# Decay rows of an mLSTM block loaded as two half loads per head group, under a new written order

## The chip, the cores and the metric

One Trainium2 chip (trn2), one of its cores. The metric is the time of one execution on the device, in microseconds (us). Of the kernel before, three timed runs gave 303.72, 299.47 and 302.79 us: the median is 302.79 us. One more execution was profiled; its own time is given further below.

## The reference, cut to what matters

Three layers in a row: an mLSTM attention with a matrix state for each of 2 batches and 8 heads (768 steps, head size 40), a feed-forward layer on the normalised result, and a gated convolutional feed-forward layer. All in float32.

```python
for t in range(S):                                    # attention, S = 768
    m_new = np.maximum(f_gate[:, :, t] + m, i_gate[:, :, t])
    f_stab = np.exp(f_gate[:, :, t] + m - m_new)
    i_stab = np.exp(i_gate[:, :, t] - m_new)
    C = f_stab * C + i_stab * outer(vt, kt);  n = f_stab * n + i_stab * kt
    y[:, :, t] = sigmoid(o_gate) * (C @ qt) / maximum(abs(n @ qt), 1)
x = y as (2, 768, 320)
x = x + relu(layernorm(x) * g @ w_ch1) @ w_ch2        # 320 -> 1280 -> 320
h = relu(x @ w_in)                                    # 320 -> 1024
out = (h * sigmoid(conv3(h, conv_w))) @ w_out         # 1024 -> 320
```

## The kernel before, in words

The sequence is cut into six chunks of 128 steps (c = 0 to 5). Within a chunk the recurrence is a masked attention, and what came before it enters through a carried state, so a chunk of a batch b is one "group" (c, b). Three stages run as a pipeline over chunks: the attention of chunk c, the first feed-forward layer f1 of chunk c (five units u, L605), and the second layer f2 of chunk c - 3 (L666).

A group (c, b) in `attention` (L415) does, in the order of its code:

- L420 loads the block `vk` (values, keys, output gate; 484 KB) and L431 the block `xy` (keys and queries, 512 KB). Both have three buffers that go around.
- For c >= 2, L451 loads the weights `wt` of the group from the small DRAM tensor `gd` (gate sums, written once at L337) by broadcasting eight rows to 128 partitions (512 KB); POOL masks it (L453) and ACT takes eight exponentials (L457).
- For c >= 2, L472 and L473 load `eg`, the decay rows, also from `gd`: partitions 0 to 63 get four rows of 128 numbers (heads 0 to 3 of the batch), partitions 64 to 127 the next four. The source is an access pattern of two blocks of 64 equal rows, and it is one load (256 KB, 128 pieces of 2,048 B). ACT takes its exponential in place (L474). `eg` has two buffers, one for each batch. For c = 1 the rows come from TensorE instead (L467, L470).
- POOL multiplies the queries by `eg` (L476, tile `qt`), and later the carried state by the last column of `eg` (L565, tile `ctmp`). After these two the buffer of `eg` is free for the group (c + 1, b).
- TensorE makes the scores (L491), VectorE multiplies them by `wt` (L498), TensorE makes numerator and norm from state and values (L517, L520), and the keys' product for the new state (L558); VectorE adds that to `ctmp` (L566), which is the state of (c + 1, b).
- VectorE and ACT normalise, and TensorE transposes the result (L579) for f1. An f1 unit is sixteen matmuls (L592 to L596), a relu on ACT (L616), a remainder on VectorE (L618) and twelve matmuls (L601 to L603). f2 is built of the same two helpers.

The order of all work is written out by hand. `Sched` (L84) only collects the operations in the order of the code and numbers them, 0 to 1294. `ORDER` (L32) is a list of these numbers, and the instructions are emitted in that order; a "-" in it is a dummy matmul on TensorE (L805), of which there are 52. If the list is no permutation, or if it breaks a dependency, the order of the code is used (L132). Each engine works off its own instructions strictly in this order. All loads and stores go out through one queue, SP's (L256 for loads): an issue that waits there, for a buffer to come free, holds back every later issue. Weights come in 640 KB blocks (L357) through staging buffers, are put together by ACT, VectorE and POOL (L343 to L346) and split in two parts (L369 to L391).

Of the kernel before, what the change touches and what calls it, by code (L numbers as in the profile page):

```python
# [13 lines left out]
AF = mybir.ActivationFunctionType  # L14
# [3 lines left out]
L = 128  # L18
# [11 lines left out]


ORDER = """  # L32
13 6 12 11 4 10 5 38 82 29 2 37 28 8 15 91 98 16 27 3 9 17 19 20 21 18 22 107 25 23 26 - - - - - - - - - - - - - -
49 24 163 30 84 164 14 83 32 31 85 114 39 33 86 34 46 40 87 41 47 48 42 88 - - - 52 43 36 50 44 51 92 35 53 54 93 55
7 56 - - - - 67 94 57 45 62 99 63 95 74 100 58 59 60 64 68 65 89 66 61 96 - - - - - - - 76 101 165 108 90 69 123 109
70 102 287 71 166 168 167 72 103 169 97 73 77 - - - - - - - - - - - - - - - - 79 110 130 171 170 80 299 0 78 111 173
298 115 81 - - - - - - 175 286 - - 292 177 116 174 184 172 388 176 104 112 288 105 75 113 256 289 106 146 124 117
# [43 lines left out]
"""  # L81


# [58 lines left out]
def tile_kernel(ctx, tc, gf, gf80, kq0, vko, gln, w1, w2, win, wout, cw, out):  # L142
# [5 lines left out]
    op = sch.op  # L148
# [58 lines left out]
    ctmp = ctm[0:104, 0:164].rearrange("p (j e) -> p j e", j=4)  # L207
    negm = ctm[:, 0:256].bitcast(BF16).rearrange("p (k t) -> p k t", k=4)
# [38 lines left out]
    def da(n, psum=False):  # L247
        return 120 + (0 if psum else 45) + 0.72 * n

    def dg(n):  # L250
        return 80 + 2.3 * n
# [163 lines left out]
    def attention(c, b, to_xt):  # L415
# [43 lines left out]
        if c:  # L459
            if c == 1:  # L460
                gk, gb = pbank("sm")

                def feg():
                    for j in range(4):
                        for h2 in range(2):
                            r = r0 + 4 * h2 + j
                            pe.matmul(out=gb[64 * h2:64 * h2 + 64, j * L:(j + 1) * L], rhs=g80[0:16], start=True, stop=True,  # L467
                                      lhsT=ident[0:16, r:r + 1].to_broadcast([16, 64]))
                op(P, 1036, ["g80", "ident"], [gk], feg, act=0.5)
                op(A, da(512, True), [gk], [ek], lambda: ac.activation(out=e, in_=gb.rearrange("p (j t) -> p j t", j=4), func=AF.Exp))  # L470
            else:
                gsrc = gd[r1:r1 + 8, :].rearrange("(i j) t -> i (j t)", i=2).unsqueeze(1).to_broadcast([2, 64, 4 * L])  # L472
                load(e, gsrc, [ek], 128 * 2048 + 1, reads=["gd"])  # L473
                op(A, da(512), [], [ek], lambda: ac.activation(out=e, in_=e, func=AF.Exp))  # L474
            op(G, dg(512), [ek, (xkk, 0), (xkk, 1)], [qk],
               lambda: gq.tensor_tensor(out=q[0:104], in0=xt[0:104, 1, :].rearrange("p (j t) -> p j t", j=4), in1=e[0:104], op=ALU.mult))  # L476
        if c < NC - 1:
            op(A, 130, [(wk, h) for h in range(8)], [dk], lambda: ac.activation(out=d.unsqueeze(2), in_=w[:, :, L - 1:L], func=AF.Copy))
# [69 lines left out]
        if c < NC - 1:  # L548
# [12 lines left out]
            if c == 0:  # L561
                op(V, dv(164), [sk], [ck], lambda: ve.tensor_copy(out=cb[0:104], in_=sv))
            else:
                op(G, dg(164), [ek, ck], ["ctmp", "negm"],
                   lambda: gq.tensor_tensor(out=ctmp, in0=cb[0:104], in1=e[0:104, :, L - 1:L].to_broadcast([104, 4, D + 1]), op=ALU.mult))  # L565
                op(V, dv(164), [sk, "ctmp"], [ck], lambda: ve.tensor_tensor(out=cb[0:104], in0=sv, in1=ctmp, op=ALU.add))  # L566
        yield
# [300 lines left out]
```

## Time and profile of the kernel before

| what | value |
|---|---|
| timed runs, us | 303.72, 299.47, 302.79; median 302.79 |
| the profiled execution, us | 299.37 |
| its span, first to last instruction, us | 297.6 |
| TensorE busy (matmul) | 277.1 us, 93% |
| VectorE, ACT, POOL busy | 193.1 us, 178.7 us, 101.7 us |
| bytes moved by DMA | 33.17 MB, 111 GB/s over the span |
| mean granted TensorE clock | 0.986 |

How to read it: 297.6 us is the time between the first and the last instruction, and 1.8 us of the execution lie outside it. TensorE's share counts the dummies too, and the ends of matmuls are modelled, so "busy" can hide small waits. The clock is a share of full speed, 1.00 being 2.4 GHz. In the rows, PE is TensorE, PEld its weight loads, DVE VectorE, ACT ScalarE, POOL GpSimd, SP the queue that issues DMA.

### The profile page before, as it was taken

Reading aid. Unit: us, or ns where it says so; the run is one execution under the profiler, and the core shown is the slowest. Engines: PE = TensorE matmul, PEld = TensorE weight load, DVE = VectorE, ACT = ScalarE, POOL = GpSimd, SP = SyncE. Lnnn points to the kernel's source line nnn. Section 1 sums busy time; section 2 is a strip of 40 time slices with the busy share of each in tenths; the row PEclk is TensorE's granted clock in tenths of the full one; section 3 lists DMA queues with packets and bytes.
Section 4 is the critical chain, followed back from the end, with each engine's and each line's share of the span. In section 5 each row is a group of like instructions: output and inputs, shape, how many; then the busy total and the mean of one; then the engine's idle time right before and its main releaser. Section 6 shows DMA issues by size and latency. Waiting matters only on the chain.

```text
span 297.6 us, 7323 instructions
## 1 busy us (share of the span) xinstructions
PE 277.1 (93%) x2972; PEld 254.6 (86%) x2975; DVE 193.1 (65%) x415; ACT 178.7 (60%) x409; POOL 101.7 (34%) x152
## 2 busy tenths in 40 slices
PE   8999999898985797979999799999999999999995
PEld 3756899888884796968999699999999999999994
DVE  5597579539960579656693566857354468777573
ACT  3875796776871905954555743455344347787473
POOL 2331865496543925517120060001000200434540
PEclk9999999999999599999999999999999999999998
DMA  7958746983456257300425000000001000010012
GB/s 274 343 206 319 324 162 209 312 273 107 161 173 191 94 213 224 132 31 9 166 74 154 21 0 25 24 3 0 2 0 46 0 0 2 2 40 6 2 45 88
DMA packets 10514, 33.17 MB, mean 111 GB/s; under 512 B 1216, under 2 KB 3040, under 8 KB 10480
## 3 DMA queue, kind: packets, MB, share of 16 engines
q1 hardware_dynamic: 10480, 32.71, 32.2%
q8 instruction: 23, 0.38, 0.6%
q14 instruction: 11, 0.09, 0.1%
HBM read 30.70 MB, written 2.01 MB: 110 GB/s over the span
## 4 chain that ended last, share of the span: by engine, by line
PE 59%; DMA 17%; DVE 11%; ACT 5%; issue 3%; POOL 2%; SPq 0%; DVEq 0%; POOLq 0%; ACTq 0%
DMA eg<-gd 17%; PE bk L601 7%; PE bk L603 7%; PE bk L602 7%; PE bk L592 6%; PE bk L593 6%; PE bk L594 6%; PE bk L805 3%; PE bk L491 3%; PE bk L595 3%; PE bk L596 3%; PE bk L520 2%; DVE wt L498 2%; PE bk L517 2%; DVE scr L716 1%
## 5 line engine op out<-in xcount | busy, mean ns | idle before, releaser
L716 DVE SCALAR_TENSOR_TENSOR scr<-scr,cwr 128x256 f32<-128x256 f32 x70 | 34.4, 527 | 15.3 <-ACT scr L710 15.1
L601 PE MATMUL bk<-w2h,uh 128*128 128x320 f32 x120 | 39.1, 326 | 0.0
L603 PE MATMUL bk<-w2h,ul 128*128 128x320 f32 x120 | 37.8, 315 | 0.2 <-DVE ul L618 0.2
L602 PE MATMUL bk<-w2l,uh 128*128 128x320 f32 x120 | 37.7, 314 | 0.0
L592 PE MATMUL bk<-xth,w1h 128*128 128x256 f32 x120 | 35.3, 295 | 1.9 <-DVE ul L618 1.9
L618 DVE SCALAR_TENSOR_TENSOR ul<-bk,uh 128x512 fp32r<-128x512 f32 x30 | 20.5, 686 | 22.7 <-ACT uh L616 22.4
L594 PE MATMUL bk<-xtl,w1h 128*128 128x256 f32 x120 | 33.8, 282 | 0.0
L593 PE MATMUL bk<-xth,w1l 128*128 128x256 f32 x120 | 33.7, 281 | 0.0
L592 PE MATMUL bk<-rh,wih 128*128 128x256 f32 (+1 forms) x96 | 28.2, 294 | 2.5 <-DVE ul L618 2.1
L593 PE MATMUL bk<-rh,wil 128*128 128x256 f32 (+1 forms) x96 | 27.2, 283 | 0.0
L594 PE MATMUL bk<-rl,wih 128*128 128x256 f32 (+1 forms) x96 | 27.1, 283 | 0.0
L616 ACT ACTIVATE uh<-bk 128x512 fp32r<-128x512 f32 x30 | 17.7, 590 | 15.6 <-PE bk L596 11.5
L691 POOL COPY scr<-scr 128x8 f32<-128x8 f32 (+1 forms) x21 | 4.3, 216 | 65.2 <-DVE scr L721 54.6
L592 PEld LDWEIGHTS bk<-xth,w1h 128*128 128x128 f32 x120 | 22.5, 188 | 3.1 <-DVE ul L618 2.3
L346 POOL TENSOR_TENSOR scr<-scr 128x640 int32<-128x640 int32 x14 | 18.2, 1302 | 20.4 <-DVE scr L345 15.2
L498 DVE TENSOR_TENSOR wt<-bk,wt 128x512 f32<-128x512 f32 x24 | 15.5, 684 | 13.9 <-PE bk L491 6.1
L457 ACT ACTIVATE wt<-wt,bcol 128x128 f32<-128x128 f32 x64 | 22.9, 390 | 2.4 <-POOL wt L453 2.4
L601 PEld LDWEIGHTS bk<-w2h,uh 128*128 128x128 f32 x120 | 23.1, 192 | 0.8 <-issue 0.2
L603 PEld LDWEIGHTS bk<-w2h,ul 128*128 128x128 f32 x120 | 23.1, 192 | 0.4 <-DVE ul L618 0.4
L601 PE MATMUL bk<-woh,uh 128*128 128x320 f32 x74 | 23.3, 315 | 0.0
L602 PEld LDWEIGHTS bk<-w2l,uh 128*128 128x128 f32 x120 | 23.1, 193 | 0.0
L603 PE MATMUL bk<-woh,ul 128*128 128x320 f32 x74 | 23.0, 310 | 0.0
(185 smaller groups left out, 813.9 us busy)
## 6 DMA issues: line engine op xcount, KB each, us to landing
xy<-in_kq_dram SPq DMA_DIRECT2D x12, 512.0 KB, 6.5
vk<-in_vko_dram SPq DMA_DIRECT2D x12, 484.0 KB, 8.6
wt<-gd SPq DMA_DIRECT2D x8, 512.0 KB, 3.8
scr<-in_w_dram SPq DMA_DIRECT2D x6, 640.0 KB, 6.4
stg<-in_w_dram SPq DMA_DIRECT2D x4, 640.0 KB
scr<-in_win_dram SPq DMA_DIRECT2D x4, 640.0 KB, 11.4
scr<-in_wout_dram SPq DMA_DIRECT2D x4, 640.0 KB, 4.0
eg<-gd SPq DMA_DIRECT2D x8, 256.0 KB
```

The source lines that it names most:

```text
L346: op(G, 80 + 1.78 * n, [(rk, 0)], [(rk, 1)], lambda: gq.tensor_tensor(out=hi, in0=hi, in1=lo, op=ALU.add))
L457: lambda h=h: ac.activation(out=w[:, h, :], in_=w[:, h, :], func=AF.Exp, bias=bcol[:, c * 16 + r0 + h:c * 16 + r0 + h + 1]))
L498: lambda wv=wv, pb=pb: ve.tensor_tensor(out=wv, in0=pb.rearrange("p (h t) -> p h t", h=4), in1=wv, op=ALU.mult))
L592: pe.matmul(out=pv, lhsT=wh[:, k, fs], rhs=hi(k), start=(k == 0), stop=False)
L593: pe.matmul(out=pv, lhsT=wl[:, k, fs], rhs=hi(k), start=False, stop=False)
L594: pe.matmul(out=pv, lhsT=wh[:, k, fs], rhs=lo(k), start=False, stop=False)
L601: pe.matmul(out=a, lhsT=hi(b), rhs=wh[:, k, :], start=first, stop=False)
L602: pe.matmul(out=a, lhsT=hi(b), rhs=wl[:, k, :], start=False, stop=False)
L603: pe.matmul(out=a, lhsT=lo(b), rhs=wh[:, k, :], start=False, stop=last)
L616: op(A, da(512, True), [pk], [hk], lambda: ac.activation(out=uh[i], in_=pb, func=AF.Relu))
L618: lambda: ve.scalar_tensor_tensor(out=ul[i], in0=pb, scalar=0.0, in1=uh[i].bitcast(F32), op0=ALU.max, op1=ALU.subtract))
L716: lambda k=k, j=j: ve.scalar_tensor_tensor(out=cvt()[:, j], in0=h[:, j, :, k:k + 128], scalar=cw_t[:, k, f0 + j:f0 + j + 1], in1=cvt()[:, ...
```

## The change: what it does

The load of `eg` (L473) becomes two loads of 64 partitions each, one for each half of the heads. Each takes four consecutive rows of `gd` as one row of 512 numbers and broadcasts it to 64 partitions. The tile's dependency key is split in two halves; the exponential at L474, the product at L476 and the product at L565 use both halves. Bytes, values and the two buffers stay as they are. There are eight such groups, so eight loads more; the operations are now numbered 0 to 1302, and `ORDER` is a new list of them with 54 dummies.

```diff
-            op(A, da(512, True), [gk], [ek], lambda: ...)
+            op(A, da(512, True), [gk], [(ek, 0), (ek, 1)], lambda: ...)
...
             else:
-                gsrc = gd[r1:r1 + 8, :].rearrange("(i j) t -> i (j t)", i=2).unsqueeze(1).to_broadcast([2, 64, 4 * L])
-                load(e, gsrc, [ek], 128 * 2048 + 1, reads=["gd"])
-                op(A, da(512), [], [ek], lambda: ac.activation(out=e, in_=e, func=AF.Exp))
-            op(G, dg(512), [ek, (xkk, 0), (xkk, 1)], [qk],
+                for h2 in range(2):
+                    gsrc = gd[r1 + 4 * h2:r1 + 4 * h2 + 4, :].rearrange("j t -> (j t)").partition_broadcast(64)
+                    load(e[64 * h2:64 * h2 + 64].rearrange("p j t -> p (j t)"), gsrc, [(ek, h2)], 64 * 2048 + 1, reads=["gd"])
+                op(A, da(512), [], [(ek, 0), (ek, 1)], lambda: ac.activation(out=e, in_=e, func=AF.Exp))
+            op(G, dg(512), [(ek, 0), (ek, 1), (xkk, 0), (xkk, 1)], [qk],
...
-                op(G, dg(164), [ek, ck], ["ctmp", "negm"],
+                op(G, dg(164), [(ek, 0), (ek, 1), ck], ["ctmp", "negm"],
...
-49 24 163 30 84 164 14 83 32 31 85 114 39 33 86 34 46 40 87 41 47 48 42 88 - - - 52 43 36 50 44 51 92 35 53 54 93 55
+49 24 163 30 84 164 14 83 32 31 85 114 39 33 86 46 40 34 87 41 299 47 48 42 88 - - - 52 43 36 50 44 51 92 35 53 54
...
+155 317 318 149 135 268 408 319 320 150 269 141 326 309 266 136 270 137 151 138 321 271 308 194 401 391 274 409 322
```

What the new order does with the parts that matter here, read from the two lists with the groups written as (c, b):

- Start. The new list keeps the first twelve issues of SP. The `xy` block of (1, 1) moves three places up, ahead of the third block of `w2`; the loads of `vk` for (1, 0) and (2, 0) and of the convolution's weights (L769) also come ahead of the fourth blocks of `w1` and `w2`, and that of `vk` for (1, 1) comes later. On TensorE the first f1 unit has two dummies more ahead of it, and the rest of its sequence up to the end of chunk 1 is the same but for neighbours that change places.
- SP around chunks 2 and 3. Before: `wt` (2,0), `eg` (2,0), `wt` (2,1), `vk` (2,1), `xy` (2,0), `xy` (2,1), `eg` (2,1), and later `eg` (3,1), `eg` (3,0). After: `wt` (2,0), `xy` (2,1), second half of `eg` (2,0) (number 401), `wt` (2,1), first half of `eg` (2,0) (400), both halves of (2,1) (419, 420), the first half of (3,0) (522), then `vk` of (2,1) (407). In the same way both halves of `eg` (4,0) stand ahead of `vk` (3,0).
- POOL. `ctmp` of (2,0) (number 448) moves from behind the two key products L480 of chunk 2 to a place ahead of the query product L476 of (2,1). In chunks 3 and 4 the batch 0 pairs L476 and L565 move up in a like way, ahead of the masks L453 that follow.
- ACT. The exponential L474 of a group stands behind its loads by a stretch of other work in both lists; for (3, 0), (3, 1) and (4, 0) the new one has it ahead of more of the L457 exponentials of its group than before.
- TensorE. The groups' scores, numerators and transposes come at nearly the same places among the units of f1 and f2, mostly one to four operations earlier or later; the number and the size of matmuls is the same.
- End. The units of f2 for chunks 3 to 5 change places among themselves.

## Rows read from the trace of the kernel before

**Rows 1.** Page: the granted clock in 40 slices of the span.
```profile
PEclk9999999999999599999999999999999999999998
```

**Rows 2.** Stretches: length, busy PE, PEld, DVE, ACT, POOL, clock, DMA share, GB/s.
```profile
0.00:45.00 45.00, 43.27 (x432) 30.57 (x436) 31.47 (x82) 31.47 (x62) 19.23 (x27) 1.00 0.74 271
45.00:184.00 139.00, 124.10 (x1613) 116.16 (x1615) 89.67 (x188) 83.51 (x212) 62.12 (x86) 0.98 0.42 137
184.00:290.00 106.00, 105.64 (x928) 104.56 (x915) 69.34 (x140) 61.14 (x129) 20.34 (x39) 1.00 0.04 12
97.80:104.70 6.90, 6.37 (x60) 5.81 (x60) 2.77 (x5) 6.13 (x15) 5.67 (x10) 0.51 0.28 92
```

**Rows 3.** Timeline of TensorE: start, length, instruction, idle before it and its releaser.
```profile
68.07 0.68 PE L517 MATMUL bk<-c,qt 40*64 40x41 f32 x32 [1.08 <-DVE wt L498]
...
98.33 2.08 PE L491 MATMUL bk<-xy 40*128 40x128 f32 x16 [5.28 <-DVE wt L498]
...
118.59 0.87 PE L579 MATMUL bk<-ident,xc 128*128 128x128 f32 x6 [1.35 <-DVE c L566]
...
133.50 0.39 PE L592 MATMUL bk<-rh,wih 128*128 128x260 f32 x1 [1.68 <-DVE ul L618]
...
168.59 0.39 PE L592 MATMUL bk<-xth,w1h 128*128 128x256 f32 x1 [1.43 <-DVE ul L618]
```

**Rows 4.** Timeline of ACT at three of the loads, the same columns.
```profile
65.37 0.63 ACT L474 ACTIVATE eg<-eg 128x512 f32<-128x512 f32 x1 [1.55 <-DMA eg<-gd]
...
95.25 0.63 ACT L474 ACTIVATE eg<-eg 128x512 f32<-128x512 f32 x1 [6.21 <-DMA eg<-gd]
95.78 0.58 ACT L616 ACTIVATE uh<-bk 128x512 fp32r<-128x512 f32 x1
...
130.67 0.63 ACT L474 ACTIVATE eg<-eg 128x512 f32<-128x512 f32 x1 [1.74 <-DMA eg<-gd]
...
132.15 0.57 ACT L616 ACTIVATE uh<-bk 128x512 fp32r<-128x512 f32 x1
```

**Rows 5.** Chain that ended last: start, length; first and last of four such pieces.
```profile
51.58 13.77 DMA eg<-gd
...
156.51 8.02 DMA eg<-gd
```

**Rows 6.** Busy time by stretch, as rows 2: only eg loads, only wt loads.
```profile
140.30:142.10 1.80, 1.38 (x11) 1.38 (x12) 1.80 (x6) 0.01 (x1) 0.00 (x0) 1.00 0.13 49
147.20:149.60 2.40, 2.40 (x32) 1.97 (x33) 1.35 (x4) 0.78 (x2) 1.10 (x1) 1.00 0.54 213
```

**Rows 7.** DMA issues: count, KB, us to landing; 115.5 to 135 us, then all.
```profile
xy<-in_kq_dram SPq DMA_DIRECT2D x1, 512.0 KB, 15.6
...
vk<-in_vko_dram SPq DMA_DIRECT2D x12, 484.0 KB, 8.6
wt<-gd SPq DMA_DIRECT2D x8, 512.0 KB, 3.8
...
out_dram<-scr SPq DMA_DIRECT2D x12, 160.0 KB, 1.8
```

**Rows 8.** Instructions on eg: count, ns least/median/most, first and last start.
```profile
L256 SPq DMA_DIRECT2D eg<-gd x8: 497/514/644, 43.5 to 156.5; - x8
```

**Rows 9.** Chain that ended last: a run of sixteen dummies.
```profile
20.55 3.60 PE bk L805 x16
```

**Rows 10.** Timeline of POOL and TensorE near the numerators of chunk 2.
```profile
70.19 0.46 POOL L565 TENSOR_TENSOR ctmp<-c,eg 104x164 f32<-104x164 f32 x1
...
71.70 0.68 PE L517 MATMUL bk<-c,qt 40*64 40x41 f32 x32
```

**Rows 11.** Timeline of VectorE and POOL ahead of the wait at 118.59 us.
```profile
112.98 0.54 DVE L545 SCALAR_TENSOR_TENSOR xc<-x,mv,gln 128x320 f32<-128x320 f32 x1
...
115.27 3.02 DVE L545 SCALAR_TENSOR_TENSOR xc<-x,mv,gln 128x320 f32<-128x320 f32 x1
...
115.63 1.09 POOL L453 TENSOR_SCALAR_AFFINE_SELECT wt<-wt 128x1024 f32<-128x1024 f32 x1
```

More of the change, by code (lines that the diff above doesn't have):

```diff
@@ L32 @@
 ORDER = """
-13 6 12 11 4 10 5 38 82 29 2 37 28 8 15 91 98 16 27 3 9 17 19 20 21 18 22 107 25 23 26 - - - - - - - - - - - - - -
-49 24 163 30 84 164 14 83 32 31 85 114 39 33 86 34 46 40 87 41 47 48 42 88 - - - 52 43 36 50 44 51 92 35 53 54 93 55
-7 56 - - - - 67 94 57 45 62 99 63 95 74 100 58 59 60 64 68 65 89 66 61 96 - - - - - - - 76 101 165 108 90 69 123 109
-70 102 287 71 166 168 167 72 103 169 97 73 77 - - - - - - - - - - - - - - - - 79 110 130 171 170 80 299 0 78 111 173
-298 115 81 - - - - - - 175 286 - - 292 177 116 174 184 172 388 176 104 112 288 105 75 113 256 289 106 146 124 117
[43 rows of a table removed]
+13 6 12 4 10 11 5 38 82 29 2 37 28 8 15 91 98 16 27 3 9 17 19 20 21 18 22 107 25 23 26 - - - - - - - - - - - - - -
+49 24 163 30 84 164 14 83 32 31 85 114 39 33 86 46 40 34 87 41 299 47 48 42 88 - - - 52 43 36 50 44 51 92 35 53 54
+93 - - - - 57 55 7 56 94 45 62 67 99 63 95 74 58 59 60 64 68 65 - - - - 165 89 66 90 96 61 76 123 101 178 100 69 286
+77 70 388 102 108 166 287 71 167 168 109 75 72 110 73 115 169 - - - - - - - - - - - - - - - - - - 79 170 177 78 111
+173 171 80 116 172 174 112 81 250 - - - - - - - - - - - 288 97 103 292 113 130 124 104 175 184 256 289 105 126 125
[43 rows of a table added]
 """
@@ L469, in attention @@
                 op(P, 1036, ["g80", "ident"], [gk], feg, act=0.5)
-                op(A, da(512, True), [gk], [ek], lambda: ac.activation(out=e, in_=gb.rearrange("p (j t) -> p j t", j=4), func=AF.Exp))
+                op(A, da(512, True), [gk], [(ek, 0), (ek, 1)], lambda: ac.activation(out=e, in_=gb.rearrange("p (j t) -> p j t", j=4), func=AF.Exp))
             else:
-                gsrc = gd[r1:r1 + 8, :].rearrange("(i j) t -> i (j t)", i=2).unsqueeze(1).to_broadcast([2, 64, 4 * L])
-                load(e, gsrc, [ek], 128 * 2048 + 1, reads=["gd"])
-                op(A, da(512), [], [ek], lambda: ac.activation(out=e, in_=e, func=AF.Exp))
-            op(G, dg(512), [ek, (xkk, 0), (xkk, 1)], [qk],
+                for h2 in range(2):
[3 more added lines that the diff above has]
+            op(G, dg(512), [(ek, 0), (ek, 1), (xkk, 0), (xkk, 1)], [qk],
                lambda: gq.tensor_tensor(out=q[0:104], in0=xt[0:104, 1, :].rearrange("p (j t) -> p j t", j=4), in1=e[0:104], op=ALU.mult))
```

85 rows, old and new, of the table ORDER are left out of this document.

## The prediction

> **What bounds the kernel now.** I read the page first, then the windows by stretch, then TensorE's timeline for its waits, then ACT's at the same times, and last the chain of waits and the DMA.
>
> From 184 to 290 us TensorE is busy for 105.64 of 106 us [rows 2]: nothing but its own work bounds that stretch, and the change removes no matmul. From 0 to 45 us the loads set the pace (DMA share 0.74) and dummies fill TensorE. What can be won lies between 45 and 184 us: TensorE is busy for 124.10 of 139 us, so it waits for 14.9 us [rows 2]. The granted clock shows one dip there [rows 1]: from 97.8 to 104.7 us it is 0.51, which is the 1.2 GHz level of the two, 1.2 and 2.4 GHz [rows 2], right after TensorE's longest wait, 5.28 us up to 98.33 [rows 3].
>
> Four of the twelve waits that make up the 14.9 us go back to the `eg` load. The wait of 5.28 us is for L498, which waits for ACT's exponentials; ACT had stood still for 6.21 us until `eg` landed, and its queue then began with L474 [rows 3, 4]. Likewise 1.08 us at 68.07 behind L474 at 65.37, and 1.68 us at 133.50 behind L474 at 130.67 through the relu L616 at 132.15 [rows 3, 4]. The wait of 1.43 us at 168.59 is of the same kind: L474 began only when `eg`, issued at 156.51, had landed 8.02 us later [rows 3, 5]. Together 1.08 + 5.28 + 1.68 + 1.43 = 9.47 us. The other eight sum to 14.9 - 9.47 = 5.4 us; the largest, 1.35 us at 118.59 [rows 3], has nothing to do with `eg` (rival 2).
>
> Why is the load slow? The chain that ended last holds four of these loads, 13.77 us the first and 8.02 us the last [rows 5]. While only an `eg` load was in the DMA engines their share was 0.13, which is 2 of 16, at 49 GB/s; while only a `wt` load ran it was 213 GB/s and 0.54 on the mean of a stretch with its start and tail [rows 6]. 256 KB at 49 GB/s are 5.3 us, and two groups' loads in a row 10.7 us. Others suffer as well: an `xy` load issued right behind two `eg` loads took 15.6 us to land, against 3.8 us for a `wt` load of the same size [rows 7].
>
> **The change part by part.** *Half loads.* No row shows a load of 64 partitions. The nearest from below is an output store of 160 KB, 1.8 us, from above a `wt` load of 512 KB, 3.8 us, whose source is a broadcast of the same tensor in the same manner [rows 7]; at the far end the halves still run on two engines and the pair takes the 8.02 us of today [rows 5]. I take 2.5 us, since 128 KB is nearer to the store, and 0.5 us more for the second issue: the group lands 3 us after its first issue in place of 8 to 14.
>
> The Trainium skill, page "DMA: Bandwidth & Descriptors", section "Why a DMA increments its semaphore by 16 and not by 1", says that a load is dealt to the largest number of engines, up to 16, that divides the slowest dimension of both its sides. That is 2 for the old pattern, which the 0.13 of [rows 6] agrees with, and 16 for the new one, which no run here shows yet. Against the split speaks the page "SBUF — State Buffer", sections on the port swizzle and on issuing two DMAs to hit both halves: 64 partitions reach half of the ports, and two such loads one after the other do not add up. By its 196 GB/s for 64 partitions the pair would take an estimated 1.3 us in the engines, where its 436 GB/s for all ports would give 0.6; that is under 1 us for a group, and the sum would stay within 1 us of what follows unless several of these stood on the path.
>
> *What goes.* The four waits, 9.47 us, and the dip of the clock behind the longest one: 6.9 us at 0.51 did what takes 6.9 x 0.51 = 3.5 us, so 3.4 us. Together 12.9 us. Bounds: 0, if the load was not the last to come, and 14.9 + 3.4 = 18.3 us, if no wait at all is left.
>
> *What is late next.* In the place of each removed wait the next latest thing shows. The other eight waits have a mean of 5.4 / 8 = 0.68 us; four of these are 2.7 us. Bounds 0 and 9.47.
>
> *Added issues.* Eight more issues on SP, each of about 0.51 us [rows 8], 4 us in all. SP only issues and nothing computes on it, so they are hidden unless a load is due within half a microsecond; then 0.5 us each, 4 us at most, less than nothing if a half lands before its partner did. I take 0. The exponential's second semaphore and the doubled keys add nothing to ACT and POOL: the same instructions run.
>
> *Dummies.* Two more ahead of the first f1 unit. Sixteen in a row take 3.60 us, so 0.225 us each [rows 9]: 0.45 us if that stretch waits for them, 0 if it waits for loads anyway. I take 0.45.
>
> *The new order at the start and the end.* Up to 45 us the loads set the pace, at 271 GB/s [rows 2]. Some blocks change places; about 1 MB put ahead of a needed block (`vk` and `xy`, 996 KB) delays it by 1.0 MB / 271 GB/s = 3.8 us, and the needed one put ahead gains as much. From both sides: -3.8 to +3.8 us; I take 0, since the same blocks come before the end of chunk 1 in both orders. At the end the f2 units change places on a TensorE that is busy for 99.7% [rows 2]: 0, give or take 1 us.
>
> Sum, on the profiled execution: 299.37 - 12.9 + 2.7 + 0.45 = 289.6 us. The three timed runs lie 0.1 to 4.35 us above the profiled execution's 299.37 us, their median 3.4 us. Some of that spread may be the clock's dip itself, so I add half of it, 1.7 us: 291.3 us, 3.8% under 302.79. About 2% either way, 6 us, is what a measurement of this kernel tells from no change.
>
> **The rivals.** *1. The split does not spread.* The pair stays on two engines, 8.02 us or more a group [rows 5]. For it: no row shows such a load. Against: `wt` is broadcast in the same manner and is fast [rows 7]. Then only the new order and the dummies count: 299.37 + 0.45 + 1.7 = 301.5 us.
>
> *2. The load hid other waits.* With `eg` early, ACT, VectorE and POOL are as late. For it: ACT was busy for 6.13 of 6.9 us after the long wait [rows 2], so much of its work was only waiting its turn; and one VectorE instruction, L545, took 3.02 us against 0.54 when POOL's L453 and its neighbours ran beside it, after which TensorE waited 1.35 us [rows 3, 11]; the new order puts POOL's products in other places and may make more of these. Against: in its 6.21 us ACT had nothing else to do [rows 4], so that work does move up. If half of the 9.47 us stays and the clock still dips behind the longest one: 299.37 - 4.7 + 0.45 + 1.7 = 296.8 us, just at 2%.
>
> *3. SP is blocked, and it ends slower.* In the new order the first half of `eg` (3,0) is issued ahead of `vk` (2,1), and both halves of (4,0) ahead of `vk` (3,0). These halves wait until POOL has done L565 of the group before, which frees the buffer; `vk` is queued behind them, and the numerator L517 waits for `vk`. For it: before, L565 of (2,0) ran at 70.19 us, only 1.5 us ahead of L517 of (2,1) at 71.70 [rows 10], and a `vk` load takes 8.6 us [rows 7]. At that lateness `vk` lands at 70.65 + 0.5 + 8.6 = 79.7 us, TensorE waits 8 us, and the clock falls behind it as it did before: 8 + 3.4 = 11.4 us a place, two places 22.8 us: 291.3 + 22.8 = 314.1 us; at one place alone 302.7 us. It decides when L565 starts later than some 9 us before its numerator. Against: the new list has POOL do L565 of (2,0) ahead of the second query product, thus well ahead of the numerators, and with the two busy engines gone a `vk` load should take nearer to 4 us (the `wt` row) than 8.6.
>
> **How the numbers follow.** Forecast 0.62, rival 1 0.06, rival 2 0.19, rival 3 0.13 (0.08 at two places, 0.05 at one). Faster by over 2% (under 296.7 us): 0.62 and half of rival 2, 0.71. Within 2%: rival 1, the other half of rival 2, rival 3 at one place, 0.06 + 0.09 + 0.05 = 0.20, and 0.01 for an unlucky start: 0.21. Slower: rival 3 at two places, 0.08. The range: at the low end all waits and the dip are gone, 299.37 - 18.3 + 0.45 = 281.5, and half a microsecond for what lies outside, 282; at the high end it takes in rivals 1 and 2, 302. What is left out is rival 3 and a lucky start below 282, under 2 in 10.
>
> **What would show each step.** Right: the `eg` loads land within about 3 us, `xy` and `vk` in 4 to 6; the chain of waits holds no piece of 8 us for `eg`; the window from 45 us until the attention of chunk 5 is over has TensorE waits of 6 to 9 us in all; the clock has no dip to 0.5 there; ACT nowhere stands still for 6 us until `eg` lands. Wrong: TensorE waits ended by `vk`, or by VectorE's L498 behind a late `wt`; a low clock behind a new wait; landings of `eg` still at 8 us with a DMA share of 0.13; or a first f1 unit that starts several microseconds later than before.

## The result, and the profile after

The changed kernel took 285.42 us (median of four runs, 284.53 to 287.46), against 302.15 us for the kernel before in the same series (299.47 to 303.72). The ratio is 0.946, with a 95% interval from 0.938 to 0.955: faster by some 5%. The profiled execution took 287.46 us, its span is 285.7 us. The forecast was 291.3 us.

In the rows of the changed kernel, line numbers behind L473 are one higher than before (the exponential is L475, the query product L477, scores L492, numerators L518 and L521, transposes L580).

The page of the changed kernel: engines' busy time, the granted clock in 40 slices, the chain that ended last, and the issues of `eg`. These answer to the table ahead of the prediction and to [rows 1, 5, 7].

```profile
span 285.7 us, 7333 instructions
...
PE 274.7 (96%) x2975; PEld 254.2 (89%) x2977; DVE 190.4 (67%) x415; ACT 178.7 (63%) x409; POOL 102.7 (36%) x152
...
PEclk9998999979999999999999999999999999999999
...
PE 82%; DVE 13%; ACT 2%; issue 2%; POOL 0%; DVEq 0%
...
vk<-in_vko_dram SPq DMA_DIRECT2D x12, 484.0 KB, 6.1
...
eg<-gd SPq DMA_DIRECT2D x16, 128.0 KB, 4.0
```

The chain that ended last had four pieces of 8 to 15 us in which it only waited for `eg`; now no DMA is in it at all, and TensorE's part is 82% (59% before). A half load lands 4.0 us after its issue (median), a `vk` load after 6.1 us where it took 8.6.

TensorE's timeline of the changed kernel, every wait over 0.3 us between 45 and 184 us; it answers to [rows 3].

```profile
57.88 1.37 PE L580 MATMUL bk<-ident,xc 128*128 128x128 f32 x6 [1.86 <-DVE c L567]
...
77.85 0.82 PE L559 MATMUL bk<-vk 128*40 128x41 f32 x32 [0.87 <-DVE x L534]
...
87.39 0.55 PE L580 MATMUL bk<-ident,x 128*128 128x128 f32 x3 [0.66 <-DVE xtl L585]
...
111.79 0.55 PE L580 MATMUL bk<-ident,xc 128*128 128x128 f32 x3 [0.38 <-DVE c L567]
```

Busy time by stretch of the changed kernel, columns as in [rows 2].

```profile
0.00:45.00 45.00, 42.48 (x424) 29.41 (x427) 30.87 (x79) 30.44 (x62) 19.51 (x28) 0.96 0.77 274
45.00:184.00 139.00, 135.03 (x1823) 128.35 (x1822) 99.66 (x220) 91.32 (x228) 61.62 (x86) 0.99 0.42 137
...
58.10:61.50 3.40, 3.40 (x17) 3.40 (x16) 1.46 (x4) 1.78 (x7) 0.00 (x0) 0.50 0.02 5
```

Between 45 and 184 us TensorE now waits for 139 - 135.03 = 4.0 us, where it was 14.9 [rows 2]. None of the four waits that go back to `eg` is left. That is the 10.9 us of which the span's 297.6 - 285.7 = 11.9 us mostly consist. The dip of the clock behind the long wait is gone too, but this execution has two others, one of 3.4 us at 0.50 among the dummies and one, in the last row, behind the wait of 1.86 us. Two of the other three runs had a mean clock of 1.00 and took 285.79 and 284.53 us.

### The profile page after: what moved, and what is told of

Same layout as the page of the kernel before. It is cut to its first block, busy times and chain, and to the rows that moved or that the text cites. A ratio compares the mean times of both kernels' runs of the same rounds, so it can differ in the third digit from the quotient of the medians.

```text
span 285.7 us, 7333 instructions
## 1 busy us (share of the span) xinstructions
PE 274.7 (96%) x2975; PEld 254.2 (89%) x2977; DVE 190.4 (67%) x415; ACT 178.7 (63%) x409; POOL 102.7 (36%) x152
## 4 chain that ended last, share of the span: by engine, by line
PE 82%; DVE 13%; ACT 2%; issue 2%; POOL 0%; DVEq 0%
PE bk L602 10%; PE bk L604 10%; PE bk L603 9%; PE bk L593 8%; PE bk L595 8%; PE bk L594 8%; PE bk L806 5%; PE bk L492 4%; PE bk L596 4%; PE bk L597 4%; PE bk L521 3%; PE bk L580 3%; PE bk L518 2%; DVE xc L546 1%; DVE wih L380 1%
## 5 line engine op out<-in xcount | busy, mean ns | idle before, releaser
L717 DVE SCALAR_TENSOR_TENSOR scr<-scr,cwr 128x256 f32<-128x256 f32 x70 | 33.7, 516 | 17.0 <-ACT scr L711 16.8
L604 PE MATMUL bk<-w2h,ul 128*128 128x320 f32 x120 | 37.2, 310 | 0.0
L692 POOL COPY scr<-scr 128x8 f32<-128x8 f32 (+1 forms) x21 | 7.5, 362 | 67.4 <-DVE scr L722 56.8
L499 DVE TENSOR_TENSOR wt<-bk,wt 128x512 f32<-128x512 f32 x24 | 15.6, 684 | 11.7 <-PE bk L492 11.5
L594 PEld LDWEIGHTS bk<-xth,w1l 128*128 128x128 f32 x120 | 22.9, 191 | 0.0
L457 ACT ACTIVATE wt<-wt,bcol 128x128 f32<-128x128 f32 x64 | 22.4, 396 | 0.9 <-POOL wt L453 0.8
L595 PEld LDWEIGHTS bk<-xtl,w1h 128*128 128x128 f32 x120 | 22.9, 191 | 0.0
```

What stands on the lines that cost most here:

```text
L457: lambda h=h: ac.activation(out=w[:, h, :], in_=w[:, h, :], func=AF.Exp, bias=bcol[:, c * 16 + r0 + h:c * 16 + r0 + h + 1]))
L499: lambda wv=wv, pb=pb: ve.tensor_tensor(out=wv, in0=pb.rearrange("p (h t) -> p h t", h=4), in1=wv, op=ALU.mult))
L594: pe.matmul(out=pv, lhsT=wl[:, k, fs], rhs=hi(k), start=False, stop=False)
L595: pe.matmul(out=pv, lhsT=wh[:, k, fs], rhs=lo(k), start=False, stop=False)
L604: pe.matmul(out=a, lhsT=lo(b), rhs=wh[:, k, :], start=False, stop=last)
L717: lambda k=k, j=j: ve.scalar_tensor_tensor(out=cvt()[:, j], in0=h[:, j, :, k:k + 128], scalar=cw_t[:, k, f0 + j:f0 + j + 1], in1=cvt()[:, ...
```

## The experiments

Theory A: the cause is that the old load runs on two DMA engines. Theory B: the cause is the new order. Theory C: it helps to have two loads, whatever their engines.

**e1: the new order with the old load.** Both places of a pair stay in the order; the one load is issued at the earlier of them, the other place is empty.

```diff
+                first = {(2, 0): 1, (2, 1): 0, (3, 0): 0, (3, 1): 1, (4, 0): 1, (4, 1): 0, (5, 0): 0, (5, 1): 1}[c, b]
                 for h2 in range(2):
-                    gsrc = gd[r1 + 4 * h2:r1 + 4 * h2 + 4, :].rearrange("j t -> (j t)").partition_broadcast(64)
-                    load(e[64 * h2:64 * h2 + 64].rearrange("p j t -> p (j t)"), gsrc, [(ek, h2)], 64 * 2048 + 1, reads=["gd"])
+                    gsrc = gd[r1:r1 + 8, :].rearrange("(i j) t -> i (j t)", i=2).unsqueeze(1).to_broadcast([2, 64, 4 * L])
+                    op(SP, 460, ["gd"], [(ek, h2)], (lambda gsrc=gsrc: sp.dma_start(out=e, in_=gsrc)) if h2 == first else (lambda: None), ...)
```

> The new order, with each pair of half loads put back to the one old load of 128 partitions (issued where the first half stands; the other place is left empty). Theory A, the load's two DMA engines are the cause: most of the gain is lost, 297 to 304 us, with TensorE waits of over 8 us between 45 us and the end of chunk 5's attention and ACT waiting for the decay rows. Theory B, the new order is the cause: 285 to 290 us. Both in part: about 292 us.

Measured: 290.27 us, ratio 0.969 (0.964 to 0.973). Well over half of the gain is there with the old load. Theory A as stated falls: the slow load alone is not what costs the time. One piece of `eg` is left in the chain that ended last, where there were four: ACT stood still until it landed, and TensorE waited behind that. ACT, then TensorE, in e1 (lines two higher than in the changed kernel):

```profile
63.90 0.63 ACT L477 ACTIVATE eg<-eg 128x512 f32<-128x512 f32 x1 [2.99 <-DMA eg<-gd]
```

```profile
68.80 0.68 PE L520 MATMUL bk<-c,qt 40*64 40x41 f32 x32 [2.26 <-DVE wt L501]
```

**e2: the old order with the half loads,** both issued one behind the other in the old load's place.

```diff
-                load(e, gsrc, [ek], 128 * 2048 + 1, reads=["gd"])
+                def halves():
+                    for h2 in range(2):
+                        gsrc = gd[r1 + 4 * h2:r1 + 4 * h2 + 4, :].rearrange("j t -> (j t)").partition_broadcast(64)
+                        sp.dma_start(out=e[64 * h2:64 * h2 + 64].rearrange("p j t -> p (j t)"), in_=gsrc)
+                op(SP, 460, ["gd"], [ek], halves, dma=128 * 2048 + 1)
```

> The old order, with both half loads issued one right after the other in the place of the old load. Theory A: 285 to 291 us, the four TensorE waits at 68, 98, 133 and 169 us (9.5 us in all) gone or under 1 us each, and no dip of the clock behind the second. Theory B: 298 to 304 us.

Measured: 288.41 us, ratio 0.961 (0.956 to 0.966). Theory B as stated falls as well: either part alone gives the larger part of the gain. TensorE's timeline of e2 (lines three higher than in the changed kernel), from 85 to 135 us:

```profile
90.04 1.16 PE L495 MATMUL bk<-xy 40*128 40x128 f32 x16 [1.14 <-DVE rl L588]
...
107.19 0.38 PE L596 MATMUL bk<-xth,w1h 128*128 128x256 f32 x1 [0.52 <-DVE ul L622]
...
111.60 0.88 PE L583 MATMUL bk<-ident,xc 128*128 128x128 f32 x6 [1.35 <-DVE c L570]
...
120.99 0.41 PE L607 MATMUL bk<-w2h,ul 128*128 128x320 f32 x1 [0.16 <-DVE ul L622]
...
131.94 0.39 PE L596 MATMUL bk<-rh,wih 128*128 128x260 f32 x1 [0.44 <-DVE ul L622]
```

The wait of 1.35 us stands at the same transposes as in [rows 3], unchanged, and the kernel before had the other four of these too, each within 0.02 us. Between the first two rows it also had the wait of 5.28 us; that is gone, and of the four `eg` waits none is left. This is the clean test of the prediction's list of causes.

**e3: the changed kernel, with each half load on two engines.** The source has the same 64 equal rows, written as two blocks of 32.

```diff
-....rearrange("j t -> (j t)").partition_broadcast(64)
+....rearrange("j t -> (j t)").unsqueeze(0).unsqueeze(0).to_broadcast([2, 32, 4 * L])
```

> The changed kernel, but each half load reads a source pattern of two blocks of 32 equal rows in place of 64 equal rows: the same two loads, bytes and pieces of 2,048 B. Theory A, with the slowest dimension of the pattern setting the number of engines: two engines again, DMA share 0.13 while only such a load runs, and 295 to 304 us. Theory C, that it is the split into two loads which helps, whatever their engines: 284 to 288 us. If the two blocks are joined on the way the share is near 1 and the time that of the changed kernel.

Measured: 297.82 us, ratio 0.995 (0.992 to 0.998). Theory C falls: two loads without more engines bring nearly nothing. The stretch of e3 in which only such loads ran, then a wait of TensorE, then the load in the chain that it followed:

```profile
151.30:156.40 5.10, 3.12 (x25) 2.87 (x23) 1.93 (x5) 1.38 (x4) 1.14 (x1) 1.00 0.13 51
```

```profile
158.13 0.58 PE L593 MATMUL bk<-rh,wih 128*128 128x260 f32 x1 [3.71 <-ACT scr L693]
```

```profile
146.01 11.06 DMA eg<-gd
```

A share of 0.13 is 2 of 16 engines, as in [rows 6], at 51 GB/s. The last half was issued at 146.01 us, behind two others on the same two engines, took 11.06 us, and TensorE waited.

**e6: e1 with the load at the later place.** The only difference to e1 is which of the two places is empty.

```diff
-... if h2 == first else (lambda: None)
+... if h2 != first else (lambda: None)
```

> The new order with the one old load, now issued where the later of the two halves stands, up to some 20 us later for the groups of chunk 5. If the new order helps because it issues the decay rows earlier: 295 to 299 us, like the two halves on two engines, with a TensorE wait of over 3 us before the scores of chunk 5. If it helps by the other operations' places: 290 us as with the earlier place.

Measured: 298.53 us, ratio 1.003 (0.999 to 1.007). So the 3% of the new order in e1 hangs on the place of this one load. Whether the rest of the order brings something by itself is not shown: e6 does not put the loads back at their old places, it issues some earlier and some later than the kernel before. SP's timeline of e1, then the same stretch of e6 (whose profiled execution was 3 us longer than its median):

```profile
126.20 0.51 SPq L475 DMA_DIRECT2D eg<-gd  x1
...
143.12 0.51 SPq L475 DMA_DIRECT2D eg<-gd  x1
```

```profile
144.01 1.58 SPq L475 DMA_DIRECT2D eg<-gd  x2
```

In e1 the load for group (5,0) goes out at 126.20 us and that for (5,1) at 143.12. In e6 both go out from 144.01 us on, side by side, and queue up on the two engines. TensorE then waits in e6 for ACT, which stood still for 4.64 us until the second had landed:

```profile
161.63 0.58 PE L595 MATMUL bk<-rh,wih 128*128 128x260 f32 x1 [7.01 <-ACT scr L695]
```

**e9: the old order with half loads on two engines,** that is e2 with the source of e3. It completes the square: either order, either number of engines.

```diff
-    gsrc = gd[...].rearrange("j t -> (j t)").partition_broadcast(64)
+    gsrc = gd[...].rearrange("j t -> (j t)").unsqueeze(0).unsqueeze(0).to_broadcast([2, 32, 4 * L])
```

> The old order with both half loads in the old load's place, each with a source of two blocks of 32 rows, so on two DMA engines if the number follows the slowest dimension. If the gain of the half loads in the old order (0.961) is that of sixteen engines: the time of the kernel before, 295 to 302 us, with the long TensorE wait at about 98 us back. If it is that of two separate loads: 286 to 291 us.

Measured: 308.24 us, ratio 1.027 (1.020 to 1.034): the gain of e2 is that of the engines. It is even slower than the kernel before, which neither side expected. In TensorE's timeline of e9 the long wait is back, and longer:

```profile
102.62 2.08 PE L495 MATMUL bk<-xy 40*128 40x128 f32 x16 [7.32 <-DVE wt L502]
...
177.23 0.58 PE L596 MATMUL bk<-xth,w1h 128*128 128x256 f32 x1 [3.19 <-DVE ul L622]
```

```profile
98.50:108.70 10.20, 6.08 (x51) 5.52 (x52) 4.73 (x7) 8.68 (x20) 7.16 (x12) 0.50 0.22 82
```

The last row, a stretch of e9, shows its price in the clock: 10.2 us at 0.50 around that wait, where it was 6.9 us at 0.51 [rows 2]. The page of e9 shows three more low stretches, where [rows 1] has that one alone:

```profile
PEclk9999999997999599995999979999999999999999
```

The two loads also take longer than the one on as many engines. From 85 to 88 us only pieces of `eg` loads moved in e9, at the same share of 0.13 but at 29 GB/s, where it was 49 [rows 6]:

```profile
85.00:88.00 3.00, 3.00 (x25) 2.92 (x24) 1.22 (x3) 3.00 (x7) 0.98 (x2) 1.00 0.13 29
```

Why the pieces went slower is open.

**e10: four engines.** As e3, with four blocks of 16 rows.

```diff
-....to_broadcast([2, 32, 4 * L])
+....to_broadcast([4, 16, 4 * L])
```

> The changed kernel with sources of four blocks of 16 rows: four engines, so 16 pieces on each and about half of the time of a load on two (2.7 us where two engines took some 2.7 to 5.4). If what counts is that the loads of two groups no longer queue up into the time when they are needed: 285 to 288 us, near the changed kernel. If every microsecond of a load is on the path: half way between 285 and 298, 291 us.

Measured: 284.85 us, ratio 0.947 (0.941 to 0.953), which is the time of the changed kernel. A stretch of e10 in which such loads ran and the last few pieces of an `xy` load, and one of the changed kernel, at the start of two half loads:

```profile
143.00:144.40 1.40, 1.40 (x13) 1.40 (x12) 0.65 (x2) 1.16 (x3) 0.00 (x0) 1.00 0.26 99
```

```profile
89.40:90.60 1.20, 1.20 (x12) 1.20 (x11) 0.73 (x2) 1.20 (x5) 1.20 (x2) 1.00 0.66 138
```

Two blocks give a share of 0.13 and four blocks 0.26, which are 2 and 4 of 16 engines; 64 rows in one block give 0.66 on the mean of a stretch with its start, which is more than ten. So the number of engines rises with the outermost count of the source. The Trainium skill, page "DMA: Bandwidth & Descriptors", section "Why a DMA increments its semaphore by 16 and not by 1", gives the largest number up to 16 that divides the slowest dimension of both sides, here 2, 4 and 16; the first two shares agree with it, and the third is no contradiction. But the time does not go on falling with the number of engines: at 99 GB/s the load is short enough.

**e4: quarter loads.** The changed kernel with four loads of 32 partitions for a group.

```diff
-                    load(e[64 * h2:64 * h2 + 64].rearrange("p j t -> p (j t)"), gsrc, ...)
+                        for k in range(2):
+                            p = 64 * h2 + 32 * k
+                            sp.dma_start(out=e[p:p + 32].rearrange("p j t -> p (j t)"), in_=row.partition_broadcast(32))
```

> The changed kernel with each half load split once more, four loads of 32 partitions for a group: 16 more issues of about 0.45 us on SP. If issues and fixed costs of a load are hidden, as the prediction has it: 284.5 to 288 us, like the changed kernel. If they stand on the path: 16 x 0.45 = 7 us more, 292 us.

Measured: 285.90 us, ratio 0.953 (0.947 to 0.960), with single runs from 283.51 to 287.50. Sixteen more issues cost nothing that shows.

**e5: the changed kernel again,** beside e6, e7 and e8.

> The changed kernel itself, beside the others of this call: 284 to 287 us, a ratio of 0.947 to 0.956 to the kernel before. With the new order alone at 0.969 and the half loads alone at 0.961, adding up would give 1 - 0.031 - 0.039 = 0.930, and one cause that both remove would give 0.961 or just under it.

Measured: 284.90 us, ratio 0.959 (0.954 to 0.964); the kernel before ran at 298.14 us in that series. The two gains don't add: with 0.969 (e1) and 0.961 (e2) for the parts, both together are about what the half loads alone give, or 1% more.

**e7: values first.** The changed kernel with `vk` of (2,1) and (3,0) moved ahead of the `eg` loads that stand before them in the order: number 407 ahead of 522, and 510 ahead of 725.

```diff
-... 283 422 411 522 413 407 429 ...
+... 283 422 411 407 522 413 429 ...
...
-375 356 725 532 520 724 465 480 510 543 ...
+375 356 510 725 532 520 724 465 480 543 ...
```

> The changed kernel with the value blocks of groups (2,1) and (3,0) issued ahead of the decay rows that wait for POOL. Rival 3 of the prediction, that SP held by these waits costs time: 1 to 4 us faster than the changed kernel. If it costs nothing, since the values still land before their numerator: the same time within 0.5%.

Measured: 285.53 us, ratio 0.961 (0.956 to 0.966), against 284.90 us for e5. SP's timeline of the changed kernel shows the wait that stands ahead of `vk` there:

```profile
49.58 15.21 SPq L256 DMA_DIRECT2D eg<-gd  x4
64.88 0.54 SPq L256 DMA_DIRECT2D vk<-in_vko_dram  x1
```

Four issues of some 0.45 us each took 15.21 us: SP stood at the half load of (3,0) until about 64.3 us, and `vk` of (2,1) came out only at 64.88. In e7 it goes out some 10 us earlier, and the time is no shorter: the late issue cost nothing that shows. The same load in e7:

```profile
54.36 0.54 SPq L256 DMA_DIRECT2D vk<-in_vko_dram  x1
```

**e8: one remainder on VectorE.** The changed kernel; L391's remainder of the fourth `w2` block moves from POOL to VectorE.

```diff
-            split_out(w2, lambda: w2h, lambda: w2l, "w2", n, V if n < 2 else G)
+            split_out(w2, lambda: w2h, lambda: w2l, "w2", n, V if n in (0, 1, 3) else G)
```

> The changed kernel with one remainder of w2 (its fourth block, 128 x 640) taken by VectorE in place of POOL, so that POOL no longer runs it beside VectorE's L546. If that overlap is what holds L546 (1.4 us each in place of 0.54) and with it TensorE's wait of 1.86 us at 57.9 us: that wait falls to about 0.7 us and the low clock that followed it in the profile is gone, 282 to 285 us. If not: 285 to 287 us.

Measured: 283.26 us (282.85 to 284.27), ratio 0.953 (0.948 to 0.958). Beside e5's 284.90 us (283.82 to 286.94) that is 0.6% less; the two ranges and the intervals of the ratios overlap, so the size is not well known. The timelines show that the mechanism is the one named. The changed kernel first, VectorE and POOL:

```profile
54.70 2.89 DVE L546 SCALAR_TENSOR_TENSOR xc<-x,mv,gln 128x320 f32<-128x320 f32 x2
57.51 0.32 DVE L567 TENSOR_TENSOR c<-bk,ctmp 104x164 f32<-104x164 f32 x1
...
54.34 1.60 POOL L391 TENSOR_TENSOR w2l<-scr,w2h 128x640 fp32r<-128x640 f32 x1
...
56.03 1.21 POOL L453 TENSOR_SCALAR_AFFINE_SELECT wt<-wt 128x1024 f32<-128x1024 f32 x1
```

and e8, VectorE alone:

```profile
53.98 1.01 DVE L546 SCALAR_TENSOR_TENSOR xc<-x,mv,gln 128x320 f32<-128x320 f32 x2
54.91 0.32 DVE L567 TENSOR_TENSOR c<-bk,ctmp 104x164 f32<-104x164 f32 x1
55.15 0.82 DVE L391 TENSOR_TENSOR w2l<-scr,w2h 128x640 fp32r<-128x640 f32 x1
```

Two L546 took 2.89 us beside POOL's two instructions. With L391 gone from POOL they took 1.01 us and were through before POOL's next one, L453, began at 55.88 us. The profiled execution of e5, the changed kernel once more, lies between the two: there L453 began only at 56.60 us, so that L391 alone ran beside them, they took 2.08 us, and TensorE waited 1.04 us. Their line in the chain of e5 that ended last:

```profile
54.62 2.08 DVE xc L546 x2
```

In e8, TensorE's wait at 57.88 us is gone altogether, not only shortened, and its busy time from 45 to 184 us is the second number of this row:

```profile
45.00:184.00 139.00, 137.28 (x1853) 130.56 (x1852) 99.59 (x225) 93.39 (x233) 59.99 (x89) 1.00 0.40 136
```

So 1.7 us of waits are left. e8 has the lowest median of the kernels that were run, though by less than these runs tell apart.

The square, as ratios to the kernel before (the changed kernel's two series gave 0.946 and 0.959; the kernel before itself ran between 298.1 and 302.2 us in the median, which is where they differ):

| | old order | new order |
|---|---|---|
| one load, two engines | 1 (the kernel before) | 0.969 at the earlier place (e1), 1.003 at the later (e6) |
| two loads, two engines | 1.027 (e9) | 0.995 (e3) |
| two loads, four engines | | 0.947 (e10) |
| two loads, sixteen engines | 0.961 (e2) | 0.946, 0.959 (the change) |

The reading that stands: `eg` was late at four places because its load was slow and because it was issued late, with the next group's load queued behind it on the same two engines. Issuing it earlier takes most of that away (e1); making it short takes all of it away in either order (e2, the change). The two share one gain, so they don't add.

## Why the prediction was right, point by point

- *Where the time lay: right.* The gain came out of the stretch from 45 to 184 us, where 14.9 us of waits became 4.0.
- *Which waits: right, and shown.* The four `eg` waits, 9.47 us, are gone in the changed kernel and in e2, where the order is the old one and the others stayed nearly as they were (one of 0.78 us became 1.81 us, one of 0.49 us went).
- *The half loads: direction right, size a little off.* 3 us from the first issue was taken for the pair; a half lands 4.0 us after its issue in the median, 2.8 us at the least. e10, with loads on four engines and the same time, shows that this size did not matter.
- *"Others suffer": right, but for less than the 15.6 us.* Of these, 5.30 us are the issue itself, which SP's timeline of the kernel before shows:

```profile
116.27 5.30 SPq L256 DMA_DIRECT2D xy<-in_kq_dram  x1
```

- *What is late next: over-sized.* 2.7 us was put in the place of the removed waits. In e2 TensorE's waits from 45 to 184 us sum to 139 - 132.96 = 6.0 us, of which 5.4 us were there before: what came in their place is 0.6 us.

```profile
45.00:184.00 139.00, 132.96 (x1800) 125.45 (x1800) 100.35 (x211) 88.04 (x222) 62.87 (x87) 0.99 0.42 139
```

- *The clock: right on the mean, not in its place.* The dip behind the long wait went; the profiled execution had two new ones, and the faster runs none to speak of.
- *Dummies and the start: nearly right.* The first f1 unit begins at 28.58 to 30.26 us (median 29.56) in the nine profiled executions with the new order, and at 28.43, 28.69 and 29.02 us in the three with the old one: 0.9 us later, where 0.45 was put.
- *The signs that it named: mixed.* The pieces of 8 us in the chain and ACT's standstill for `eg` are gone. But `eg` lands in 4.0 us and not in 3, `xy` and `vk` take 6.1 us each where 4 to 6 was named, the waits sum to 4.0 us where 6 to 9 was named, and a dip of the clock is there.
- *The step from the profile to the median: wrong in sign.* The profiled execution of the kernel before was faster than all three timed runs, and 1.7 us was added for that. The changed kernel's profiled execution was its slowest run: its median lies 2.0 us below. Of the 291.3 - 285.4 = 5.9 us by which the forecast was too high, 2.1 us lie in the own time of the profiled execution (289.6 against 287.46) and 1.7 + 2.0 = 3.7 us in this step.
- *The new order: taken as 0, and that holds only beside short loads.* With the old load it is worth 3% (e1), and that only with the early place of `eg` (e6). The prediction saw that the list issues these loads earlier, and used it only as the danger of rival 3.
- *Rival 1, no spread: did not happen.* Its time, 301.5 us or 0.4% under the median, was near the ratio of e3, 0.995. But its reason, that then only the dummies count, was incomplete: e1 and e6 show that beside slow loads the early place gains and the late one loses, and in e3 a group has one half at each. That the two cancel there is argued, not shown.
- *Rival 2, other waits: small.* VectorE held up beside POOL does cost in the new order, 1.86 us at one place (1.04 us in e5's execution), and e8 takes it away. It was a fifth of the 9.47 us that went, not half.
- *Rival 3, SP blocked: the wait came, the price did not.* SP stood for 15 us with `vk` behind, and moving `vk` ahead changed nothing (e7). L566 of (2,0) ran at 63.85 us, and the numerator of (2,1) at 73.21 us: 9.4 us ahead, on the harmless side of the 9 us that the prediction named. The two rows are of the changed kernel:

```profile
63.85 0.47 POOL L566 TENSOR_TENSOR ctmp<-c,eg 104x164 f32<-104x164 f32 x1
```

```profile
73.21 0.61 PE bk L518 x32
```

- *Half the partitions, half the ports.* The Trainium skill, page "SBUF — State Buffer", section on the port swizzle, has 64 partitions reach half of the ports, which the prediction put at under 1 us for a group. No run here measures the ports, and nothing of that shows in the time: half loads on four engines (e10), half loads on more than ten (the change) and quarter loads (e4) end about 1 us from each other.

## What to carry to other kernels

Here a broadcast load whose outermost count is two ran on two of sixteen engines, and the DMA share of a stretch where only it ran says so (0.13); written with an outermost count of four or more, as two loads, it stopped being late and holding up the rest. Before crediting such a gain to one part of a change, run each part alone: here early issue and short load each gave most of it, and they did not add. When waits behind one cause are removed, look at what is already early rather than assume an average wait in their place.

## What the runs showed that was not expected

Two loads on two engines were slower than one load of the same bytes on two engines in the old order (e9, 1.027), with `eg` pieces of 9.21 to 15.34 us in its chain against 8.02 to 14.94 us before. From 85 to 88 us their pieces went at 29 GB/s in place of 49, and more low stretches of the clock came with the longer waits; why the pieces went slower is open.

The clock: waits of TensorE of 5.28 us, 7.32 us (e9) and 3.71 us (e3) each went with a stretch at 0.50 or 0.51. Behind a wait of 1.86 us it fell in the changed kernel, and behind one of 1.88 us in e4 and in e7 it did not:

```profile
56.65 0.88 PE L586 MATMUL bk<-ident,xc 128*128 128x128 f32 x6 [1.88 <-DVE c L573]
```

is e4's, whose page gives the clock as

```profile
PEclk9999999999999999999999999999999999999999
```

The runs of the changed kernel alone have mean clocks from 0.988 to 1.00. So single runs of one kernel differ by dips, of some 1.7 us each (half of 3.4 us), that the schedule alone does not decide.
